# Two token tiles ahead of the first weight half, and the first K products formed half by half

## The chip, the cores and the metric

The kernel runs on one core of one Trainium2 chip. The metric is the device time of one execution in microseconds (us). Each run also has a span (first to last instruction on the core) and a mean granted clock of TensorE, 1.000 being full speed.

## The reference, cut to what matters

```
h  = x  + attention(layernorm(x))        # S = 2048 tokens, D = 1024
h2 = h  + ffn(layernorm(h))              # F = 3584
attention: qkv = layernorm(x) @ wqkv; 32 heads; phi(t) = where(t > 0, t + 1, exp(t)) + 1e-6
           kv = sum over tokens of phi(k)^T v; o = phi(q) kv / (phi(q) z); o @ wo
ffn:       relu(h W_gate) * (h W_up) @ W_down
```

Only the beginning matters here: layernorm of x, K = layernorm(x) @ wk, V = layernorm(x) @ wv.

## The kernel before: the parts that matter

The 16 tiles of 128 tokens are numbered here in the order in which they are processed. Four tiles make a unit. For each tile, `ln_T` computes statistics on VectorE, two tiny functions on ScalarE (Ln, Exp), a "bias" -mean*rstd on VectorE (128x1), the normalised tile `xn` on ScalarE, and its transpose `xT`, by TensorE for the first tiles and by a transposing DMA for the others.

Unit 0 is done with plain matmuls: first K of its four tiles (`k_plain`), then V of its four tiles (`v_plain`). From unit 1 on, a unit is done by Strassen's scheme (`k_unit`, then `v_unit`), which needs sums of its transposed tiles ("left sums", VectorE, of type f16) and sums of the weights ("right sums").

```
        load_x(atiles[0])                # 256 KB, one token tile, rows of 2 KB
        load_w(wk_sb, 0, D)              # 1 MB, left 512 columns of wk, pieces of 1 KB: "K-left"
        load_x(atiles[1])
        load_w(wk_sb, 1, D)              # "K-right"
        load_x(atiles[2])
        load_x(atiles[3])
        for j in range(2):
            load_w(wv_sb, j, 2 * D)
        # ... cut
        def transpose_in(t, xn):
            s, i, r = place(t)
            for k in range(2):
                pt = pspool.tile([P, KH, P], BF16, tag="D", bufs=1, name="tp")   # one PSUM buffer
                for kc in range(KH):
                    nc.tensor.transpose(pt[:, kc, :], xn[:, (k * KH + kc) * P:(k * KH + kc + 1) * P], ident[:])
                (nc.scalar.copy if k else nc.vector.tensor_copy)(
                    out=xT[s][i][:, k * KH:(k + 1) * KH, r:r + P], in_=pt[:])
        # ... cut
        with tc.high_priority():
            # ... SPIN matmuls on zeros, then
            ln_T(atiles[0])
        ln_T(atiles[1])
        todo = atiles[2:8]
        for t in units[0]:
            k_plain(t)                   # both halves of the tile's K
            ln_T(todo.pop(0))
        new_v(0)
        for n, t in enumerate(units[0]):
            v_plain(t)
            if todo:
                ln_T(todo.pop(0))
            if n == 1:
                sums_unit(1)             # left sums of unit 1
                k_sums()                 # right sums of wk
        for u in range(1, NU):
            # ... k_unit(u), with ln_T of the next unit's tiles between its steps;
            # ... u == 1: right sums of wv; kv products of unit u-1; v_unit(u), with the left sums of unit u+1
```

A scheduler decides in which order the instructions of each engine are issued, by times of its own. What is written above only limits it.

Of the kernel before, what the change touches and what calls it, by code (L numbers as in the profile page):

```python
# [7 lines left out]
ACT = mybir.ActivationFunctionType  # L8
ALU = mybir.AluOpType
FP32 = mybir.dt.float32  # L10
BF16 = mybir.dt.bfloat16
# [20 lines left out]
def block_kernel(ctx: ExitStack, tc: tile.TileContext, x, wqkv, wo, wg, wu, wd, out, H: int):  # L32
    nc = tc.nc
    P = 128
    xf = x.flatten_outer_dims()
    of = out.flatten_outer_dims()
    S, D = xf.shape
# [6 lines left out]
    NW = 512  # L44
# [3 lines left out]
    KH = KC // 2  # L48
# [45 lines left out]
    bwork = pqctx.enter_context(tc.tile_pool(name="bwork", bufs=2, side="right"))  # L94
# [32 lines left out]
    def right_ops(w, t):  # L127

        (b11, b12), (b21, b22) = [[w[:, k * KH:(k + 1) * KH, j * NW:(j + 1) * NW] for j in range(2)] for k in range(2)]
        t1, t2, t4, t3 = t[:, 0], t[:, 1], t[:, 2], b12.bitcast(FP16)  # L130

        def sums():
            nc.vector.tensor_tensor(out=t1, in0=b12, in1=b11, op=ALU.subtract)
            nc.vector.tensor_tensor(out=t2, in0=b22, in1=t1, op=ALU.subtract)
            nc.vector.tensor_tensor(out=t3, in0=b22, in1=b12, op=ALU.subtract)
            nc.vector.tensor_tensor(out=t4, in0=b21, in1=t2, op=ALU.subtract)

        return (b11, b21, b22, t4, t1, t2, t3), sums
# [88 lines left out]
    pspool = psctx.enter_context(tc.tile_pool(name="ps", bufs=1, space=PSUM))  # L227
    with ExitStack() as actx:
# [11 lines left out]
        def load_x(t):  # L240
            x_sb = bwork.tile([P, D], BF16, tag=("x_res", "oT")[atiles.index(t) % 2], bufs=XB, name="x_sb")
            nc.sync.dma_start(out=x_sb[:], in_=xf[t * P:(t + 1) * P, :])
            x_tiles[t] = x_sb

        def load_w(dst, j, col):
            nc.sync.dma_start(out=dst[:, :, j * NW:(j + 1) * NW], in_=wqkv_v[:, :, col + j * NW:col + (j + 1) * NW])

        def place(t):
            i, r = divmod(t * P, HS)
            s, r = divmod(r, SW)  # L250
            return s, i, r
# [2 lines left out]
        units = [[2 * u + v + i * ST // 2 for i in range(2) for v in range(2)] for u in range(ST // 4)]  # L254
        atiles = [t for u in units for t in u]
        load_x(atiles[0])
        load_w(wk_sb, 0, D)
        load_x(atiles[1])
        load_w(wk_sb, 1, D)
        load_x(atiles[2])  # L260
        load_x(atiles[3])
        for j in range(2):
            load_w(wv_sb, j, 2 * D)

        def ln_T(t):
            if t not in x_tiles:
                load_x(t)
            x_sb = x_tiles.pop(t)
            s, i, r = place(t)
            stats = asmall.tile([P, 2, nc.vector.BN_STATS_DIM], FP32, tag="stats", name="stats")  # L270
            for k in range(2):
                nc.vector.bn_stats(out=stats[:, k, :], in_=x_sb[:, k * NW:(k + 1) * NW])
            mv = asmall.tile([P, nc.vector.BN_AGGR_DIM], FP32, tag="mv", name="mv")
            nc.vector.bn_aggr(out=mv[:], in_=stats[:])
            sm = asmall.tile([P, 3], FP32, tag="sma", name="sma")
            lnv, rstd, nmr = (sm[:, k:k + 1] for k in range(3))
            nc.scalar.activation(out=lnv, in_=mv[:, 1:2], func=ACT.Ln, bias=LN_EPS, scale=1.0)
            nc.scalar.activation(out=rstd, in_=lnv, func=ACT.Exp, scale=-0.5)
            xn = bwork.tile([P, D], BF16, tag="hn", bufs=HB, name="xn")
            if t == atiles[0]:  # L280
                for k in range(2):
                    ks = slice(k * NW, (k + 1) * NW)
                    nc.vector.tensor_scalar(out=xn[:, ks], in0=x_sb[:, ks], scalar1=mv[:, 0:1], scalar2=rstd,
                                            op0=ALU.subtract, op1=ALU.mult)
                transpose_in(t, xn)
                return
            nc.vector.scalar_tensor_tensor(out=nmr, in0=mv[:, 0:1], scalar=-1.0, in1=rstd, op0=ALU.mult, op1=ALU.mult)
            nc.scalar.activation(out=xn[:], in_=x_sb[:], func=ACT.Identity, bias=nmr, scale=rstd)
            if t not in atiles[:PE_T]:
                nc.sync.dma_start_transpose(out=xT[s][i][:, :, r:r + P], in_=xn[:])  # L290
                return
            transpose_in(t, xn)

        def transpose_in(t, xn):
            s, i, r = place(t)
            for k in range(2):
                pt = pspool.tile([P, KH, P], BF16, tag="D", bufs=1, name="tp")
                for kc in range(KH):
                    nc.tensor.transpose(pt[:, kc, :], xn[:, (k * KH + kc) * P:(k * KH + kc + 1) * P], ident[:])
                (nc.scalar.copy if k else nc.vector.tensor_copy)(  # L300
                    out=xT[s][i][:, k * KH:(k + 1) * KH, r:r + P], in_=pt[:])

        rk, k_sums = right_ops(wk_sb, tk)
# [16 lines left out]
        def new_pk(t):  # L320
            slot = atiles.index(t) % KC
            pk[t] = wo_mem[:, slot * D:(slot + 1) * D]
# [13 lines left out]

            return token_unit(u, rk, fin)

        def k_plain(t):
            s, i, r = place(t)  # L340
            new_pk(t)
            e = bwork.tile([P, D], BF16, tag="o_sb", name="e")
            for j in range(2):
                js = slice(j * NW, (j + 1) * NW)
                ps = pspool.tile([P, NW], FP32, tag="AE"[j], bufs=2, name="kp")
                for kc in range(KC):
                    nc.tensor.matmul(ps[:], lhsT=xT[s][i][:, kc, r:r + P], rhs=wk_sb[:, kc, js],
                                     start=(kc == 0), stop=(kc == KC - 1))
                nc.scalar.activation(out=e[:, js], in_=ps[:], func=ACT.Exp)
                nc.vector.tensor_scalar(out=e[:, js], in0=e[:, js], scalar1=1.0, scalar2=PHI_EPS,  # L350
                                        op0=ALU.min, op1=ALU.add)
                nc.vector.scalar_tensor_tensor(out=pk[t][:, js], in0=ps[:], scalar=0.0, in1=e[:, js],
                                               op0=ALU.max, op1=ALU.add)

        def new_v(u):
            for t in units[u]:
                vs[t] = awork.tile([P, KC, NDW], BF16, tag="v_sb", bufs=5, name="v_sb")
                nc.gpsimd.memset(vs[t][:, :, P:NDW], 1.0)

        def v_plain(t):  # L360
            s, i, r = place(t)
            for j in range(2):
                ps = pspool.tile([P, NW], FP32, tag="AE"[j], bufs=2, name="vp")
                for kc in range(KC):
                    nc.tensor.matmul(ps[:], lhsT=xT[s][i][:, kc, r:r + P], rhs=wv_sb[:, kc, j * NW:(j + 1) * NW],
                                     start=(kc == 0), stop=(kc == KC - 1))
                nc.scalar.copy(out=vs[t][:, j * KH:(j + 1) * KH, 0:P], in_=ps[:].rearrange("p (c e) -> p c e", e=P))
# [21 lines left out]
        def sums_unit(u):  # L389
            s, _, r = place(units[u][0])  # L390
            left_sums(xT[s], xS[s], slice(r, r + 2 * P), nc.vector)
# [3 lines left out]
        with tc.high_priority():  # L395
# [3 lines left out]
            for n in range(SPIN):  # L399
                nc.tensor.matmul(spin[:], lhsT=zero[:, 0:P], rhs=zero[:], start=True, stop=True)  # L400
            ln_T(atiles[0])
        ln_T(atiles[1])
        todo = atiles[2:8]
        for t in units[0]:
            k_plain(t)
            ln_T(todo.pop(0))
        new_v(0)
        for n, t in enumerate(units[0]):
            v_plain(t)
            if todo:  # L410
                ln_T(todo.pop(0))
            if n == 1:
                sums_unit(1)
                k_sums()
        for u in range(1, NU):
            todo = atiles[4 * u + 4:4 * u + 8]
            for _ in k_unit(u):
# [19 lines left out]
        for c in range(KC):  # L437
            bnk, i = divmod(c, GPB)
            nc.vector.tensor_tensor(out=kvz[:, c, :], in0=kv_ps[bnk][:, i * NDW:(i + 1) * NDW],
                                    in1=mask[:], op=ALU.mult)  # L440
# [159 lines left out]
    last = rest[-2:]  # L600
# [314 lines left out]
    prv, k = None, 0  # L915
    for r, (wt, f, fi, toks) in enumerate(runs):
        w = [ops() for _, ops in now]
        later = []
        for n, s in enumerate(toks):
            first = n == 0 and isinstance(wt, int) and fi == 0  # L920
# [50 lines left out]
            if k == nwin - 3:  # L971
                for x in range(2):
                    t = wpools[1].tile([P, KC * 2 * GP * P], BF16, tag=("wg", "wu")[x], name="wd")
# [16 lines left out]
    for n in range(2):  # L990
        t = fpool.tile([P, 4 * D], BF16, tag="wraw", bufs=2, name="xd")
# [346 lines left out]
@with_exitstack  # L1338
def kernel(
    ctx: ExitStack,  # L1340
    tc: tile.TileContext,
    A_x: bass.AP,
    A_wqkv: bass.AP,
    A_wo: bass.AP,
    B_x: bass.AP,
    B_W_gate: bass.AP,
    B_W_up: bass.AP,
    B_W_down: bass.AP,
    out: bass.AP,
):  # L1350
    block_kernel(tc, A_x, A_wqkv, A_wo, B_W_gate, B_W_up, B_W_down, out, H=32)
# [30 lines left out]
```

## Time and profile before

| | |
|---|---|
| time, first three runs | 740.93 us median (740.51 to 741.72) |
| time, six more runs beside the changed kernel | 740.58 us median (739.56 to 741.72) |
| span of the profiled run | 739.5 us |
| first K matmul, first V matmul | 9.96 us, 27.29 us |
| V stage of unit 0 | 27.29 to 41.10 us: 13.81 us |
| K matmuls of unit 1 | 41.10 to 56.59 us: 15.49 us |

Head of the page and busy time of each engine:

```profile
span 739.5 us, 10552 instructions
PE 724.0 (98%) x3967; PEld 382.7 (52%) x4020; DVE 563.7 (76%) x992; ACT 321.5 (43%) x580; POOL 5.6 (1%) x44
```

TensorE (PE) is busy 98% of the span, so a start of some 30 us can give back a few microseconds at most. The timeline of TensorE before; the columns are start, duration, engine, line, operation, output and inputs, count, and in brackets the idle time before it with what ended it:

```profile
7.09 0.39 PE L299 MATMUL tp<-ident,xn 128*128 128x128 bf16 x4
...
9.58 0.58 PE L299 MATMUL tp<-ident,xn 128*128 128x128 bf16 x4 [2.10 <-DVE xT L300]
9.96 3.18 PE L347 MATMUL kp<-pq_mem,xT 128*128 128x512 bf16 x7
...
27.29 0.38 PE L365 MATMUL vp<-wv_sb,xT 128*128 128x512 bf16 x1
```

TensorE waits 2.10 us for VectorE's copy of the first half of tile 0. The seven K matmuls from 9.96 take 3.18 us, about twice what eight of them take elsewhere (1.89 us). The view by stretches of time before says why; its columns are the stretch, its length, busy time and count on PE, weight loads, VectorE (DVE), ScalarE (ACT) and POOL, then the granted clock, the DMA engines' busy share and GB/s:

```profile
2.50:3.50 1.00, 1.00 (x4) 0.39 (x3) 0.00 (x0) 0.00 (x0) 0.07 (x2) 1.00 0.96 352
3.50:4.50 1.00, 1.00 (x3) 0.30 (x2) 0.80 (x2) 0.00 (x0) 0.00 (x0) 1.00 1.08 383
4.50:5.50 1.00, 1.00 (x4) 0.38 (x3) 0.69 (x2) 0.20 (x2) 0.00 (x0) 1.00 1.06 351
...
9.60:13.00 3.40, 3.40 (x12) 1.48 (x12) 1.38 (x2) 1.82 (x3) 0.00 (x0) 0.50 1.07 362
48.00:54.00 6.00, 5.67 (x28) 2.58 (x27) 6.00 (x14) 4.13 (x8) 0.00 (x0) 1.00 0.33 66
54.00:58.00 4.00, 3.95 (x42) 2.80 (x42) 4.00 (x11) 3.94 (x7) 0.50 (x4) 1.00 0.43 97
```

From 9.6 to 13.0 the granted clock was 0.50. The first three rows show the loads running at 351 to 383 GB/s.

The last piece of before that the argument needs is the middle of unit 1, as the timeline shows it on all engines (SPq is the queue that issues the transposing DMAs):

```profile
38.50 0.22 DVE L287 SCALAR_TENSOR_TENSOR sma<-mv,sma 128x1 f32<-128x1 f32 x2
...
41.91 1.32 SPq L290 DMA_TRANSPOSE xT<-xn  x1
...
43.38 0.16 DVE L287 SCALAR_TENSOR_TENSOR sma<-mv,sma 128x1 f32<-128x1 f32 x1
...
44.84 7.22 SPq L290 DMA_TRANSPOSE xT<-xn  x2
...
48.77 0.69 DVE L117 TENSOR_TENSOR xS<-xT 128x1024 f16<-128x1024 bf16 x1
49.37 0.16 DVE L287 SCALAR_TENSOR_TENSOR sma<-mv,sma 128x1 f32<-128x1 f32 x1
...
49.56 1.24 ACT L288 ACTIVATE xn<-x_sb,sma 128x1024 bf16<-128x1024 bf16 x1 [1.38 <-DVE sma L287]
...
51.32 1.89 PE L314 MATMUL Aq<-pq_mem,xT 128*128 128x512 f16 x8 [0.33 <-ACT u L154]
```

Read it as a chain. The biases of tiles 9 and 10 are computed at 38.50, that of tile 11 at 43.38 and that of tile 12 at 49.37. The transpose of tile 10 is issued at 41.91 and that of tile 11 at 44.84; the latter lands at 48.16. The first left sum of unit 2, which needs tiles 8 to 11 transposed, starts at 48.77 without waiting, and TensorE waits only 0.33 us.

### The profile page before, as it was taken

To read this page: it belongs to the slowest core of one execution; us is meant where nothing else is said; L and a number is where in the kernel's file an instruction comes from. 1 tells how busy PE (TensorE), PEld (TensorE's weight loads), DVE (VectorE), ACT (ScalarE), POOL (GpSimd) and SP (SyncE) were. 2 spreads that over 40 slices of the span, in tenths; PEclk is the share of its full clock that TensorE was granted. 3 is DMA by queue.
4 is the path that set the end of the run, shared out by engine and by line. 5 is a ranking of instruction groups with operands and counts; after the bars stand their busy time and mean duration, and the time that the engine had idled before them with its cause. 6 is when DMAs were issued, how large, how long until landed. Compare 5 with 4: busy or idle time off the path is not lost.

```text
span 739.5 us, 10552 instructions
## 1 busy us (share of the span) xinstructions
PE 724.0 (98%) x3967; PEld 382.7 (52%) x4020; DVE 563.7 (76%) x992; ACT 321.5 (43%) x580; POOL 5.6 (1%) x44
## 2 busy tenths in 40 slices
PE   8999999999999999999999999999999999999997
PEld 3444555444444444444444444444444458888566
DVE  5997644676798767778778777877786479996797
ACT  4877554778887644434344444444445120000000
POOL 0000000000000000000000000000000000000000
PEclk9999999999999999999999999999999999999999
DMA  9666002169987426164638359575583399987822
GB/s 315 153 145 170 1 1 67 48 149 218 237 168 181 124 73 206 43 193 134 198 117 242 110 177 283 171 219 194 170 277 121 129 398 339 331 288 299 295 76 82
DMA packets 146594, 132.02 MB, mean 179 GB/s; under 512 B 50928, under 2 KB 128112, under 8 KB 146544
## 3 DMA queue, kind: packets, MB, share of 16 engines
q1 hardware_dynamic: 135536, 123.30, 55.4%
q10 hardware_dynamic: 11008, 8.06, 3.4%
q8 instruction: 31, 0.51, 0.3%
q14 instruction: 19, 0.16, 0.1%
HBM read 79.95 MB, written 39.85 MB: 162 GB/s over the span
## 4 chain that ended last, share of the span: by engine, by line
PE 78%; DVE 8%; ACT 7%; DMA 5%; issue 1%; SPq 0%; DVEq 0%; POOL 0%; ACTq 0%
PE accA L821 22%; PE accY L821 8%; PE accX L821 8%; PE accA L1153 8%; PE Aq L314 3%; PE accA L982 3%; PE attn L557 3%; PE accX L1153 3%; PE Aq L454 3%; PE accY L1153 2%; DMA hn<-hn 2%; ACT hn L570 2%; PE Eq L314 2%; PE accY L982 2%; PE accX L982 2%
## 5 line engine op out<-in xcount | busy, mean ns | idle before, releaser
L831 ACT ACTIVATE gu<-gu 128x512 bf16<-128x512 bf16 x72 | 45.4, 631 | 131.4 <-DVE gu L830 131.4
L826 ACT COPY snap<-accA 128x1024 f32<-128x1024 f32 x72 | 72.5, 1008 | 36.4 <-PE accA L821 36.3
L821 PEld LDWEIGHTS <-tu 128*128 128x128 f16 x384 | 37.6, 98 | 45.3
L821 PEld LDWEIGHTS <-tg 128*128 128x128 f16 x384 | 37.6, 98 | 45.3
L557 PE MATMUL attn<-wo_mem,oT 128*128 128x512 bf16 x247 | 58.1, 379 | 2.3 <-DVE o_sb L534 1.0
L830 DVE TENSOR_TENSOR gu<-accY,snap 128x1024 bf16<-128x1024 f32 x36 | 43.9, 1220 | 10.0 <-ACT snap L826 10.0
L821 PE MATMUL accA<-hn,tu 128*128 128x512 f16 (+1 forms) x192 | 49.3, 379 | 0.0
L821 PE MATMUL accA<-hn,tg 128*128 128x512 f16 (+1 forms) x192 | 49.3, 379 | 0.0
L830 DVE TENSOR_TENSOR gu<-accX,snap 128x1024 bf16<-128x1024 f32 x36 | 43.9, 1219 | 6.3 <-PE accX L821 3.7
L154 ACT COPY u<-Aq 128x512 f32<-128x512 f32 x54 | 31.1, 580 | 36.2 <-PE Aq L314 19.3
L1153 PEld LDWEIGHTS <-x 128*128 128x128 f16 (+1 forms) x448 | 43.8, 98 | 5.5
L821 PEld LDWEIGHTS <-wg 128*128 128x128 bf16 x288 | 28.2, 98 | 34.0
L821 PEld LDWEIGHTS <-wu 128*128 128x128 bf16 x288 | 28.2, 98 | 34.0
L557 PEld LDWEIGHTS <-oT 128*128 128x128 bf16 x256 | 24.6, 97 | 32.2 <-issue 4.1
L834 DVE TENSOR_TENSOR hq<-gu 128x512 bf16<-128x512 bf16 x48 | 20.3, 423 | 14.3 <-ACT gu L831 14.2
L314 PEld LDWEIGHTS <-xT 128*128 128x128 bf16 (+1 forms) x192 | 18.6, 98 | 23.8 <-issue 2.4
L534 DVE TENSOR_TENSOR o_sb<-nd,rd 128x384 bf16<-128x384 f32 (+1 forms) x48 | 23.2, 509 | 8.6 <-ACT rd L533 6.6
L1153 PEld LDWEIGHTS <-xs 128*128 128x128 f16 x280 | 27.4, 98 | 3.2
L982 PEld LDWEIGHTS <-x 128*128 128x128 bf16 (+1 forms) x168 | 16.5, 98 | 19.6
L560 DVE SCALAR_TENSOR_TENSOR x_res<-attn,x_res 128x512 bf16<-128x512 f32 x32 | 22.0, 686 | 6.1 <-PE attn L557 5.9
L1159 DVE TENSOR_TENSOR snap<-accA,u 128x1024 f32<-128x1024 f32 x16 | 19.5, 1220 | 8.0 <-PE accA L1153 7.9
L821 PE MATMUL accA<-hn,wu 128*128 128x512 bf16 x96 | 24.6, 379 | 0.0
(234 smaller groups left out, 1406.1 us busy)
## 6 DMA issues: line engine op xcount, KB each, us to landing
x<-x_dram SPq DMA_DIRECT2D x17, 896.0 KB, 8.1
x_dram<-hq SPq DMA_DIRECT2D x28, 512.0 KB, 3.0
wg<-in_B_W_gate_dram SPq DMA_DIRECT2D x14, 512.0 KB, 5.1
wu<-in_B_W_up_dram SPq DMA_DIRECT2D x14, 512.0 KB, 7.3
wraw<-in_B_W_down_dram SPq DMA_DIRECT2D x14, 512.0 KB, 4.8
x_dram<-hq SPq DMA_DIRECT2D x28, 256.0 KB, 2.5
t_dram<-wt SPq DMA_DIRECT2D x28, 256.0 KB, 2.2
xd<-x_dram SPq DMA_DIRECT2D x6, 896.0 KB, 7.3
```

Source lines behind the costliest of these rows:

```text
L154: nc.scalar.copy(out=snaps[nm, v], in_=bank[v][:])
L314: nc.tensor.matmul(ps[:], lhsT=left[m - 1][:, kc, r + v * P:r + (v + 1) * P], rhs=right[m - 1][:, kc, :], start=(start and kc == 0), stop= ...
L454: nc.tensor.matmul(ps[:], lhsT=rq[m - 1][:, kc, (c + v) * P:(c + v + 1) * P], rhs=left[m - 1][:, kc, :], start=(start and kc == 0), stop=( ...
L534: nc.vector.tensor_tensor(out=ov[:, c0:c0 + n], in0=ndv[:, :, 0:P].rearrange("p k (h e) -> p k h e", h=HPC), in1=rd[:, 0:n, :].unsqueeze(3 ...
L557: nc.tensor.matmul(ps[:], lhsT=st["oT"][:, c, :], rhs=wo_sb[:, c, j * NW:(j + 1) * NW], start=(c == 0), stop=(c == KC - 1))
L560: nc.vector.scalar_tensor_tensor(out=h_sb[:, j * NW:(j + 1) * NW], in0=ps[:], scalar=1.0, in1=h_sb[:, j * NW:(j + 1) * NW], op0=ALU.mult, ...
L821: nc.tensor.matmul(ps[:, v, :], lhsT=w[v][n - 1][:, kc, :], rhs=left[n - 1][:, kc, :], start=(t is not None and kc == 0), stop=(kc == KH - ...
L826: nc.scalar.copy(out=st[nm][:], in_=halves(st["A"]))
L830: add(out=g[:], in0=halves(st[nm]), in1=st[base][:], op=ALU.add)
L831: nc.scalar.activation(out=g[:, 0, :], in_=g[:, 0, :], func=ACT.Relu)
L982: nc.tensor.matmul(ps[:, t * NW:(t + 1) * NW], lhsT=x_tile(n, s, kh)[:, f, (t0 + t) * P:(t0 + t + 1) * P], rhs=w_tile(n, kh)[:, f, :], sta ...
L1153: nc.tensor.matmul(pv[:, tt, :], lhsT=left(m)[:, f, tt * P:(tt + 1) * P], rhs=right(m)[:, f, :], start=(t is not None and f == 0 and tt % ...
```

## The change

The intent was to shorten the start. The load of the second token tile is put ahead of K-left, so that VectorE can do its statistics early. K of the first two tiles is formed left half first, so that TensorE has work while K-right is still on its way. Tile 0's two transposed halves get a PSUM buffer each and are both copied by ScalarE, so that neither waits behind VectorE's statistics. Order-only edges pin a few instructions of VectorE and ScalarE.

```
         load_x(atiles[0])
+        load_x(atiles[1])
         load_w(wk_sb, 0, D)
-        load_x(atiles[1])
+        load_x(atiles[2])
         load_w(wk_sb, 1, D)
-        load_x(atiles[2])
         load_x(atiles[3])
# ... in ln_T: xn of tile 1 in two halves; the instructions' handles are kept in `last` for the edges
+            for ks in [slice(k * NW, (k + 1) * NW) for k in range(2)] if t == atiles[1] else [slice(0, D)]:
+                nc.scalar.activation(out=xn[:, ks], in_=x_sb[:, ks], func=ACT.Identity, bias=nmr, scale=rstd)
# ... in transpose_in
-                pt = pspool.tile([P, KH, P], BF16, tag="D", bufs=1, name="tp")
+                first = t == atiles[0]
+                pt = pspool.tile([P, KH, P], BF16, tag="DE"[k and first], bufs=1 + (k and first), name="tp")
-                (nc.scalar.copy if k else nc.vector.tensor_copy)(
+                last["copy"] = (nc.scalar.copy if k or first else nc.vector.tensor_copy)(
# ... k_plain takes the halves to form; the schedule of unit 0
-        ln_T(atiles[1])
         todo = atiles[2:8]
         for t in units[0]:
-            k_plain(t)
-            ln_T(todo.pop(0))
+            if t == atiles[0]:
+                k_plain(t, [0])
+                with tc.issue_after(last["xn"].ins), tc.issue_after(last["copy"].ins):
+                    ln_T(atiles[1])
+                with tc.issue_after(last["nmr", atiles[1]].ins):
+                    ln_T(todo.pop(0))
+            elif t == atiles[1]:
+                k_plain(t, [0])
+                k_plain(atiles[0], [1])
+                k_plain(t, [1])
+                ln_T(todo.pop(0))
+            else:
+                k_plain(t)
+                ln_T(todo.pop(0))
# ... in the V stage
-                k_sums()
+                with tc.issue_after(last["nmr", atiles[2]].ins):
+                    k_sums()
```

More of the change, by code (lines that the diff above doesn't have):

```diff
@@ L263, in block_kernel @@
             load_w(wv_sb, j, 2 * D)
+        last = {}
         def ln_T(t):
@@ L282, in ln_T @@
                     ks = slice(k * NW, (k + 1) * NW)
-                    nc.vector.tensor_scalar(out=xn[:, ks], in0=x_sb[:, ks], scalar1=mv[:, 0:1], scalar2=rstd,
-                                            op0=ALU.subtract, op1=ALU.mult)
+                    last["xn"] = nc.vector.tensor_scalar(out=xn[:, ks], in0=x_sb[:, ks], scalar1=mv[:, 0:1],
+                                                         scalar2=rstd, op0=ALU.subtract, op1=ALU.mult)
                 transpose_in(t, xn)
                 return
-            nc.vector.scalar_tensor_tensor(out=nmr, in0=mv[:, 0:1], scalar=-1.0, in1=rstd, op0=ALU.mult, op1=ALU.mult)
-            nc.scalar.activation(out=xn[:], in_=x_sb[:], func=ACT.Identity, bias=nmr, scale=rstd)
+            last["nmr", t] = nc.vector.scalar_tensor_tensor(out=nmr, in0=mv[:, 0:1], scalar=-1.0, in1=rstd,
+                                                            op0=ALU.mult, op1=ALU.mult)
+            for ks in [slice(k * NW, (k + 1) * NW) for k in range(2)] if t == atiles[1] else [slice(0, D)]:
+                nc.scalar.activation(out=xn[:, ks], in_=x_sb[:, ks], func=ACT.Identity, bias=nmr, scale=rstd)
             if t not in atiles[:PE_T]:
@@ L337, in k_unit, with k_plain @@
             return token_unit(u, rk, fin)
-        def k_plain(t):
+        ke = {}
+        def k_plain(t, halves=range(2)):
             s, i, r = place(t)
-            new_pk(t)
-            e = bwork.tile([P, D], BF16, tag="o_sb", name="e")
-            for j in range(2):
+            if t not in ke:
+                new_pk(t)
+                ke[t] = bwork.tile([P, D], BF16, tag="o_sb", name="e")
+            e = ke[t]
+            for j in halves:
                 js = slice(j * NW, (j + 1) * NW)
```

## The prediction

> **What bounds the kernel.** By the page TensorE is busy 98% of a 739.5 us span; after about 74 us the chain of waits is nearly all matmuls. The change touches only the first 30 us. In the two builds every engine issues the same sequence after roughly 80 us.
>
> Where TensorE loses time at the start (timeline and windows of before):
> - Spin matmuls run until 7.26. The first half of tile 0 is transposed at 7.09 to 7.48, but VectorE copies it out only at 9.16, behind the statistics of x1 (landed 7.71; 1.29 us) and their aggregate. Both halves share one PSUM buffer, so TensorE waits 2.10 us.
> - From 9.6 to 13.0 the granted clock is 0.50; seven K matmuls start every 0.425 us instead of 0.216: 1.5 us lost. The Trainium skill ("TensorE: Matmul & The Clock Gate", Part 1) says that an idle window of about 3.4 us halves the clock and a busy one restores it. The trace agrees: idle from 7.5 to 9.6, half clock, full again at 13.0.
>
> V starts at 27.3. VectorE is busy without a gap from 13.7 to 38, nearly so to 60, and the chain runs through VectorE, ScalarE's xn and the transposing DMAs until 74. TensorE idles only 1.7 us from 27 to 74. So the gain must exist on VectorE as well as on TensorE.
>
> **What changes.**  xn of tile 1 becomes two halves (about 0.65 us each, from 1.24); tile 0's first copy goes from VectorE (0.37) to ScalarE (0.56).
> - x1 lands near 4.5 instead of 7.7. K-left comes after it, near 7.7 (was about 7.05). x2 lands near 8.4, K-right near 11.5 (was 10.8), at the measured 345 GB/s.
> - Tile 0: both transposes end near 7.9, ScalarE copies near 8.1 and 8.6, eight left matmuls start near 8.2 (was 9.96). The idle falls to about 0.5 us, so the clock should stay full.
> - VectorE: its idle from 6.5 to 13.7 is 3.5 us. In the new order I count 2.3 (1.1 for ScalarE's ln/exp behind the two copies, 1.2 for x3, which lands near 12.3 as before). With the moved copy, a lead of about 1.6 us.
> - New loss: TensorE's order puts three right matmuls of tile 0 ahead of tile 1's left ones, so it waits for K-right from about 10.2 to 11.5.
>
> Scheduling this by hand with measured durations, V starts at 25.5 to 26.3, 1.0 to 1.8 us earlier; about 1.3 us should survive to the end. Most of the 3.6 us of wait and half clock is not gained: the K-right wait and saturated VectorE take it back.
>
> **Predicted: 739.5 us**, 8 in 10 between 738.4 and 740.6. Faster by over 2%: 1%. Within 2%: 98%. Slower by over 2%: 1%.
>
> **What the profile would show.** Granted clock near 1.0 from 9 to 13; tile 0's left matmuls from about 8.2 at 0.216 us spacing; a TensorE wait ended by the K-right DMA near 11.5; VectorE without gaps from about 12.3; first V matmul at 25.5 to 26.3.
>
> **What would make it wrong.** The clock falls to half again because of the K-right wait: V moves by under 0.5 us. K-left lands later than 8.2: a loss one for one. The lead dies in the V stage or unit 1, where the transposing DMAs (about 3.1 us each) or the reordered V sums set the pace: no gain at the end. Or the pinned order saves more VectorE idle than I count: up to 2.5 us gained.

## The result, and the profile after

Ratios in this document are the mean time of one kernel's fast runs over the mean of the other's fast runs of the same rounds, so they are not quite the ratio of the medians quoted beside them. Brackets are 95% intervals. All outputs are right.

| | before | after |
|---|---|---|
| median of 6 runs each | 740.58 us | 745.22 us |
| lowest, highest | 739.56, 741.72 us | 742.93, 746.33 us |
| ratio | | 1.006 [1.0043, 1.0077] |
| first K matmul (profiled run) | 9.96 us | 8.92 us |
| first V matmul | 27.29 us | 26.36 us |
| K matmuls of unit 1 | 15.49 us | 19.50 us |

The change lost 4.6 us by the medians. It is within 2%, but far above the predicted range of 738.4 to 740.6. The changed kernel's six runs roughly follow the clock that was granted: for example 742.93 us at 1.000, 744.80 at 0.998, 745.44 at 0.997, 746.33 at 0.995.

Head of the page of the changed kernel:

```profile
span 743.0 us, 10607 instructions
PE 726.4 (98%) x4020; PEld 382.7 (52%) x4020; DVE 564.0 (76%) x991; ACT 322.9 (43%) x582; POOL 5.8 (1%) x44
```

Work is the same on every engine to within 2.4 us. (The higher count of TensorE instructions is mostly records missing from the trace of before: its 4020 weight loads had 3967 matmul records.) The timeline of TensorE after:

```profile
7.05 0.61 PE L304 MATMUL tp<-ident,xn 128*128 128x128 bf16 x8
8.92 1.89 PE L356 MATMUL kp<-pq_mem,xT 128*128 128x512 bf16 x8 [1.26 <-ACT sma L280]
...
12.61 0.81 PE L356 MATMUL kp<-pq_mem,xT 128*128 128x512 bf16 x3 [1.58 <-DMA pq_mem<-in_A_wqkv_dram]
...
26.36 1.46 PE L374 MATMUL vp<-wv_sb,xT 128*128 128x512 bf16 x6
```

The eight transposes of tile 0 now run in one go. The K matmuls then wait 1.26 us. The profile puts that wait down to ScalarE's Exp, which had long been done; the matmuls start when K-left lands, at 8.9. In a second profile of the same kernel (run e7 below) the same wait is put down to the DMA of K-left. The next wait, 1.58 us, is for K-right, which landed at 12.6.

The stretches of time after:

```profile
2.50:3.50 1.00, 1.00 (x4) 0.39 (x3) 0.15 (x1) 0.00 (x0) 0.07 (x2) 1.00 1.06 395
3.50:4.50 1.00, 1.00 (x3) 0.30 (x2) 1.00 (x2) 0.00 (x0) 0.00 (x0) 1.00 0.35 90
4.50:5.50 1.00, 1.00 (x4) 0.38 (x3) 0.46 (x3) 0.41 (x2) 0.00 (x0) 1.00 0.81 238
...
9.60:13.00 3.40, 1.82 (x12) 0.91 (x11) 1.86 (x4) 1.92 (x5) 0.00 (x0) 1.00 1.08 357
48.00:54.00 6.00, 3.48 (x20) 1.70 (x19) 3.77 (x9) 2.59 (x6) 0.00 (x0) 0.99 0.11 22
54.00:58.00 4.00, 4.00 (x12) 1.51 (x11) 2.69 (x6) 3.89 (x5) 0.00 (x0) 0.59 0.77 160
```

Three things differ. The loads fall to 90 GB/s from 3.5 to 4.5 us, where before they ran at 383. The clock stays at 1.00 from 9.6 to 13.0, as I had predicted. And from 48 to 54 TensorE stands still for 2.5 of 6 us, after which the clock is at half: 0.59 over 54 to 58, in a window that the records place at 53.9 to 57.3.

The middle of unit 1 after:

```profile
42.00 0.22 DVE L289 SCALAR_TENSOR_TENSOR sma<-mv,sma 128x1 f32<-128x1 f32 x2
...
43.45 1.23 SPq L294 DMA_TRANSPOSE xT<-xn  x1
...
45.55 8.15 SPq L294 DMA_TRANSPOSE xT<-xn  x2
...
50.40 0.69 DVE L117 TENSOR_TENSOR xS<-xT 128x1024 f16<-128x1024 bf16 x1 [2.23 <-DMA xT<-xn]
51.01 0.15 DVE L289 SCALAR_TENSOR_TENSOR sma<-mv,sma 128x1 f32<-128x1 f32 x1
...
51.20 1.24 ACT L292 ACTIVATE xn<-x_sb,sma 128x1024 bf16<-128x1024 bf16 x1 [3.12 <-DVE sma L289]
52.34 1.05 ACT L154 COPY u<-Aq 128x512 f32<-128x512 f32 x2
...
52.96 2.71 PE L319 MATMUL Aq<-pq_mem,xT 128*128 128x512 f16 x8 [2.52 <-ACT u L154]
```

The chain of before has become a block. The two biases at 42.00 are those of tiles 10 and 11: tile 10's comes 3.4 us later than before (38.57), tile 11's 1.3 us earlier (43.38). The transpose of tile 10 is issued 1.5 us later (43.45 against 41.91) and that of tile 11 0.7 us later (45.55 against 44.84). Tile 11's also took longer from issue to landing, 4.76 us against 3.33, and lands at 50.31 instead of 48.16. VectorE then reaches the first left sum of unit 2 before its tiles are transposed and waits 2.23 us. Behind it in VectorE's order stands the bias of tile 12, at 51.01. ScalarE's xn of tile 12 waits 3.12 us for that bias. Behind it in ScalarE's order stand the copies that empty TensorE's accumulators. TensorE waits 2.52 us for the copies. The bias stood behind that sum in the kernel before too (sum 48.77, bias 49.37); there the sum did not have to wait.

Where the time went, from these two traces: the first V matmul came 0.93 us earlier, the V stage took 13.81 us in both, and the K matmuls of unit 1 took 4.01 us longer. The sum, +3.1, is what the start of unit 2 shows (72.01 against 68.91), and the spans differ by 3.5. Of the 4.01, 2.2 is the longer wait (2.52 against 0.33) and about 1.7 is half of the 3.4 us window at half clock.

### The profile page after: what moved, and what is told of

The parts are those of the page before. It is cut to its first block, busy times and chain, and to the rows that moved or that the text cites. A ratio compares the mean times of both kernels' runs of the same rounds, so it can differ in the third digit from the quotient of the medians.

```text
span 743.0 us, 10607 instructions
## 1 busy us (share of the span) xinstructions
PE 726.4 (98%) x4020; PEld 382.7 (52%) x4020; DVE 564.0 (76%) x991; ACT 322.9 (43%) x582; POOL 5.8 (1%) x44
## 4 chain that ended last, share of the span: by engine, by line
PE 77%; DVE 9%; ACT 6%; DMA 5%; issue 1%; SPq 0%; DVEq 0%; POOL 0%
PE accA L842 22%; PE accY L842 8%; PE accX L842 8%; PE accA L1174 8%; PE Aq L319 4%; PE accA L1003 3%; PE accX L1174 3%; PE attn L578 3%; PE Aq L475 3%; PE accY L1174 2%; PE Eq L319 2%; ACT hn L591 2%; DMA hn<-hn 2%; PE accY L1003 2%; PE accX L1003 2%
## 5 line engine op out<-in xcount | busy, mean ns | idle before, releaser
L842 PE MATMUL accA<-hs,tg 128*128 128x512 f16 x96 | 24.6, 379 | 0.0
```

What stands on the lines that cost most here:

```text
L842: nc.tensor.matmul(ps[:, v, :], lhsT=w[v][n - 1][:, kc, :], rhs=left[n - 1][:, kc, :], start=(t is not None and kc == 0), stop=(kc == KH - ...
```

## The experiments

**Theories.** T1: the load order made the weights late, and V with them. T2: the scheduler's new order in the V stage and unit 1 made the block. T3, the rival: neither matters, the two profiles differ by the accident of where a half-clock window fell. Each can be true in part.

Several kernels pin instructions with this helper, which lays order-only edges between consecutive instructions of an engine. No wait is taken away by it.

```
+def _order_edges(tc, mark, engine, wanted):
+    traced = [i for i in tc.nc.cur_bb.bb.instructions[mark:] if i.engine == engine]
+    for first, then in wanted:
+        tc.add_manual_dep(traced[then], traced[first].name, <order only>, reason="order")
+        mark = len(tc.nc.cur_bb.bb.instructions)     # ahead of new_v(0), that is ahead of the V stage
+        _order_edges(tc, mark, VectorE, _chain([...]))     # and ScalarE, TensorE
```

Runs e1 to e4 shared one chip and its runs of before (11 runs, median 740.29 us), e5 to e8 the next (739.97), e9 to e12 the last (740.42).

### e1: the changed start with the order of before from the V stage on

```
 # the changed kernel, with
+_order_edges(..., the first 80 VectorE, 60 ScalarE and 200 TensorE instructions from the V stage on, as before had them)
```

> The changed kernel with the issue order of VectorE, ScalarE and TensorE, from the V stage on, put back to that of the kernel before by order edges; the start is the changed one. Theory A (the loss is in the order that the scheduler chose for the stage after the edited one): the first V matmul stays near 26.4, no TensorE wait of 2.5 us near 50, and the time is 739 to 740.2 us, ratio to before 0.998 to 1.000. Rival B (the new start itself costs, through loads or the earlier collisions): 743 to 746, ratio about 1.006.

Measured: 742.11 us, ratio 1.0024 [1.0007, 1.0041]. First V matmul at 27.02. K-left and K-right landed at 9.6 and 13.2, TensorE waiting 2.74 us for the first. K of unit 1 took 15.87 us and no window ran at half clock. So with the old order the block is gone. But the changed start alone does not gain; it loses. The time lies between the ranges of the two theories and meets neither.

### e2: the start of before with the changed kernel's order from the V stage on

```
 # the kernel before, with
+_order_edges(..., the same instructions, in the changed kernel's order)
```

> The kernel before with its own start, and from the V stage on the issue order of the changed kernel forced by the same kind of edges. Theory A: the loss appears without the edited start: 744 to 747 us, ratio 1.004 to 1.008, a TensorE wait of over 2 us near 51 and half clock after it. Rival B: 740 to 741.5, ratio about 1.000.

Measured: 742.56 us, ratio 1.002 [1.0004, 1.0037], again between the two expected ranges. First V matmul at 25.76. Its timeline shows the same block as the changed kernel's:

```profile
49.10 0.69 DVE L130 TENSOR_TENSOR xS<-xT 128x1024 f16<-128x1024 bf16 x1 [2.30 <-DMA xT<-xn]
...
49.90 1.24 ACT L301 ACTIVATE xn<-x_sb,sma 128x1024 bf16<-128x1024 bf16 x1 [3.18 <-DVE sma L300]
...
51.66 3.26 PE L327 MATMUL Aq<-pq_mem,xT 128*128 128x512 f16 x8 [2.59 <-ACT u L167]
```

The late order makes the block by itself, with the old start. Eight matmuls then take 3.26 us, at half clock from 52.0. Its two runs with a clock of 0.999 and more took 740.18 and 740.51 us, no longer than before; the four at 0.997 and 0.998 took 742.41 to 743.39. So the order seems to cost time mostly through the half clock that follows the wait; only one of these six runs was traced.

### e3 and e4: the block's own links

e3 moves the bias of tile 10 ahead of the last three left sums of unit 1. (In the kernel before it also stood ahead of all four right sums of wv; two of these, 46 and 47, still precede it in e3.) e4 puts the bias of tile 12 ahead of the left sum that it stood behind. Both are the changed kernel pinned to its own order but for this.

```
 # e3: VectorE's chain of the changed kernel
-[... 8, 34, 47, 9, 10, 11, 29, ...]        # 8 to 11: left sums of unit 1; 29: the bias of tile 10
+[... 8, 34, 47, 29, 9, 10, 11, ...]
 # e4
-[... 52, 63, 68, 53, 54, 55, ...]     # 52 to 55: left sums of unit 2; 63: the bias of tile 12
+[... 63, 52, 68, 53, 54, 55, ...]
```

> The changed kernel in exactly its order, but VectorE's bias of token tile 10 moved from behind the left sums of unit 1 to ahead of their second. If the late transpose of tile 10 starts the loss: its transpose issues at 42.0 to 42.6 instead of 43.45, tile 11's lands near 49 instead of 50.3, the TensorE wait near 50 falls from 2.5 to about 1.3 us, time 742 to 744. If the position of this one instruction does not matter: 744.5 to 746.

> The changed kernel in exactly its order, but VectorE's bias of token tile 12 moved one place, ahead of the first left sum of unit 2, which waits for the transposing DMA. The transposes stay as late as in the changed kernel. If the cost comes through the in-order queues (VectorE held by that sum, so ScalarE held at xn of tile 12, so its copies of the accumulators and TensorE): the 2.5 us TensorE wait falls below 0.8, the half clock near 55 is gone, time 740 to 742. If the late data itself holds TensorE: no change, 744.5 to 746.

Measured: e3 743.76 us, 1.0045 [1.0024, 1.0066]; e4 743.4 us, 1.0041 [1.0022, 1.0059]. e3 is inconclusive: its first V matmul came at 27.76 because K-left landed late (10.3), the transpose of tile 10 was issued no earlier (43.92; counted from the first V matmul, 0.9 us earlier), and TensorE still waited 2.16 us. In e4 the wait of 2.5 us is gone, so the bias of tile 12 behind the left sum did carry it. No window ran at half clock in this trace, as expected. But a wait of 1.57 us for VectorE came a few matmuls later, and the time did not fall to the expected 740 to 742. Breaking one link moves part of the wait to the next.

### e5: the load order alone

```
 # the kernel before, pinned from the start to its own order on VectorE, ScalarE and TensorE, and
         load_x(atiles[0])
+        load_x(atiles[1])
         load_w(wk_sb, 0, D)
-        load_x(atiles[1])
+        load_x(atiles[2])
         load_w(wk_sb, 1, D)
-        load_x(atiles[2])
         load_x(atiles[3])
```

> The kernel before with only its first loads reordered as in the change (x0, x1, K-left, x2, K-right, x3); the order on VectorE, ScalarE and TensorE is pinned to that of the kernel before. Theory C (the load order itself loses DMA time): between 3.5 and 6 us the traffic dips under 300 GB/s, where the two traces with the old order keep 305 to 389; K-left lands at 8.6 to 10.3 instead of 7.0, K-right at 12.3 to 14 instead of 10.5 to 10.8, the first V matmul moves to 27 to 28.5 and the time is 741.3 to 743.5. Rival (my prediction's arithmetic, K-left at 7.7 and K-right at 11.5 with steady traffic): no dip, first V matmul near 26.3, 740 to 741.

Measured: 745.39 us, ratio 1.0068 [1.0054, 1.0081]. The load order alone, in the old start, costs as much as the whole change, and more than theory C had expected (741.3 to 743.5); the traffic fell under 300 GB/s as it had expected (249 to 272 from 3.5 to 5.5 us). Its timeline of TensorE:

```profile
9.68 1.02 PE L360 MATMUL kp<-pq_mem,xT 128*128 128x512 bf16 x4 [1.18 <-DMA pq_mem<-in_A_wqkv_dram]
...
13.38 1.44 PE L360 MATMUL kp<-pq_mem,xT 128*128 128x512 bf16 x3 [2.67 <-DMA pq_mem<-in_A_wqkv_dram]
...
30.74 13.98 PE L378 MATMUL vp<-wv_sb,xT 128*128 128x512 bf16 x63
```

K-left lands at 9.6 and K-right at 13.3, and a half-clock stretch lies over 11.8 to 18.6 (by estimate, half of these 6.8 us are lost). So part of this price is the waits and part the clock; all six runs had a clock of 0.994 to 0.998. The rest of the change (K left half first, two PSUM buffers) takes back part of what its load order costs: the changed kernel's V came at 26.4, this one's at 30.7.

### e6: the left sums of unit 2 behind everything that others wait for

```
 # the changed kernel pinned to its own order, but for VectorE
-[..., 52, 63, 68, 53, 54, 55, 30, 31, ...]     # 30, 31: the adds of two accumulators
+[..., 63, 68, 30, 31, 52, 53, 54, 55, ...]
```

> The changed kernel in exactly its order, but VectorE's four left sums of unit 2, the first of which waits for the last transposing DMA, moved behind the bias of tile 12 and the two adds of the accumulators that they held up. The transposes stay as late. Theory A' (the loss in unit 1 is head-of-line blocking in the in-order queues): no TensorE wait over 0.6 us between 48 and 56, no half clock there, unit 1 takes 15.7 to 16.4 us instead of 19.5, time about 741 to 742 (what is left is the later start). If late transposes hold the data that TensorE needs: unit 1 stays above 18 us, time 744 to 746.

Measured: 744.03 us, ratio 1.0046 [1.003, 1.0062]. The median missed the expected 741 to 742. Its timeline shows the block gone, and where part of the time was given back:

```profile
49.75 1.89 PE L332 MATMUL Aq<-pq_mem,xT 128*128 128x512 f16 x8
...
59.85 1.89 PE L332 MATMUL Aq<-tv,xS 128*128 128x512 f16 x8 [1.46 <-ACT m L167]
```

K of unit 1 took 14.97 us, the shortest of all runs. Its V part took 14.79 instead of 12.3, with waits of 0.70 and 1.46 us. One of its six runs had a clock of 1.000 and took 742.0 us; the others, at 0.997 and 0.998, took up to 745.27. The profiled run shows no half clock in this stretch, so I have no trace of what lowers it in those runs.

### e7: the changed kernel again

> The changed kernel unaltered, as the reference of this chip: 744 to 746 us, a DMA dip between 3.5 and 6 us, unit 1 about 18 us long, or 19.5 where the clock halves in it; its fastest run, at clock 1.000, near 742.9.

Measured: 743.59 us (741.25 to 744.76), ratio 1.0039 [1.0022, 1.0056]. The fastest run had a clock of 1.000, the slowest 0.997. This is faster than the first set, and than the expected 744 to 746. In this trace K-left landed at 9.5 and K-right at 13.2, V started at 27.00, TensorE's wait in unit 1 was only 1.21 us and there was no half clock. The order is the same; the transpose of tile 11 took 3.45 us to land here, and 4.76 to 4.83 in the other six traces with the changed order (the changed kernel, e2, e3, e4, e6, e10). Why it takes longer in those is not shown. So V in the profiled runs of the changed start (the changed kernel, e1, e3, e4, e6, e7) spreads from 26.0 to 27.8, and the block varies from run to run.

### e8 and e10: K-left second, everything else as changed

```
 # e10: the changed kernel, and
         load_x(atiles[0])
-        load_x(atiles[1])
         load_w(wk_sb, 0, D)
+        load_x(atiles[1])
         load_x(atiles[2])
 # e8: the same, and the order of before from the V stage on, as in e1
```

> The changed kernel with the loads in the order x0, K-left, x1, x2, K-right, x3, its start otherwise in the changed order, and the later order of the kernel before (as in the run of the changed start with the old order, 742.1). Theory C: no dip, K-left lands near 7.0, the left matmuls of tile 0 start near 8.2, first V matmul at 25.2 to 25.9, time 739.3 to 740.3, so about the kernel before or 0.5 us under it. If the load order is not the cause: first V matmul near 26.5 to 27, time 741.5 to 742.5.

> The changed kernel with only the first loads in the order x0, K-left, x1, x2, K-right, x3; by the build, its instruction order on every other engine is that of the changed kernel, the late order too, and nothing is pinned. Theory C with A: no dip, first V matmul at 24.6 to 25.2 (26.1 to 27.8 in the changed kernel), 1.5 to 2.5 us gained on the changed kernel, but the late order still holds TensorE near 50: time 741 to 742.8. If the late order costs nothing once the start is early: 739.5 to 740.5. If the load order is not the cause: 743.5 to 745.

Measured: e8 740.34 us, ratio 1.0002 [0.9987, 1.0017]; e10 741.2 us, ratio 1.0005 [0.999, 1.002]; e10 is in the range of theory C with A, e8 just at the upper end of its own. In e10 the build has exactly the changed kernel's instruction order on all engines but the one that issues the loads; only this order differs. Its timeline of TensorE:

```profile
7.30 1.90 PE L356 MATMUL kp<-pq_mem,xT 128*128 128x512 bf16 x8 [0.36 <-ACT xT L305]
...
11.03 0.81 PE L356 MATMUL kp<-pq_mem,xT 128*128 128x512 bf16 x3 [0.20 <-DMA pq_mem<-in_A_wqkv_dram]
...
24.79 2.97 PE L374 MATMUL vp<-wv_sb,xT 128*128 128x512 bf16 x13
...
50.94 2.68 PE L319 MATMUL Aq<-pq_mem,xT 128*128 128x512 f16 x8 [2.58 <-ACT u L154]
```

and its loads in the second that collapsed in the changed kernel:

```profile
3.50:4.50 1.00, 1.00 (x5) 0.35 (x3) 0.78 (x2) 0.00 (x0) 0.00 (x0) 1.00 1.05 368
```

With K-left second, K-left landed at 6.6 and K-right at 11.0, the two waits shrink to 0.36 and 0.20 us, and V starts at 24.79, 1.6 to 2.2 us earlier than in the two traces of the changed kernel. The interval of e10 just misses e7's, and lies clear of that of the first set (1.0043 to 1.0077), so the loads' order costs the changed kernel about 0.3%, 2 to 3 us. But e10's block is still there, and the half clock after it (51.9 to 55.3). Here too the time followed the clock: the three runs with 0.999 and more took 740.05 to 740.44 us, the three with 0.998, the traced one among them, 741.96 to 742.99. With the old late order, e8 starts V at 24.68 and loses 1.39 us at the start of unit 1, waiting for a transposing DMA. Neither is faster than before beyond its interval: the lead at V, about 0.7 to 1.1 us against the old start without half clock (25.51 in e9, 25.76 in e2), is all or mostly spent in unit 1.

### e9: the kernel before again

> The kernel before unaltered, for a second trace of it. Theory D (the half clock at 9.6 to 13.0 in the trace that I predicted from was an accident of that execution): most runs have a granted clock of 0.999 or 1.000, the profiled one with 7 chances in 10, and then no half clock before 700 us, first V matmul near 25.8 and a span near 738.0. If the half clock belongs to the kernel: clock 0.998, first V matmul near 27.3, span 739.5 again.

Measured: 740.55 us, ratio 1.0002 [0.9989, 1.0015]. The timeline of TensorE in this second trace of the kernel before:

```profile
9.07 0.38 PE L299 MATMUL tp<-ident,xn 128*128 128x128 bf16 x4 [1.29 <-DVE xT L300]
9.29 1.73 PE L347 MATMUL kp<-pq_mem,xT 128*128 128x512 bf16 x7
...
25.51 2.32 PE L365 MATMUL vp<-wv_sb,xT 128*128 128x512 bf16 x10
```

Same program, another execution: seven matmuls in 1.73 us instead of 3.18, no half clock before the kernel's end (737.2), and V at 25.51 instead of 27.29. TensorE's wait for tile 0 was 1.29 us here and 2.10 there: x1, whose statistics VectorE does first, landed at 7.2 instead of 7.7. In each of the three sets of 11 runs of before, 9 or 10 runs had a clock of 0.999 or 1.000. The half-clock window on which I had built the prediction was an accident of the one execution that was profiled.

So the fair pair of traces is e9 and e7, the two kernels without half clock. There the changed kernel's V comes 1.49 us later (27.00 against 25.51), not earlier; unit 1's K takes 0.94 us longer (16.38 against 15.44), and the spans differ by 2.8 us (741.5 against 738.7).

### e11 and e12: why the weights are late

```
 # e11: the kernel before, pinned to its order: x0, x2, K-left, x1, K-right, x3
 # e12: the kernel before, pinned: x0, x1, K-left as two transfers (rows 0-511, 512-1023), x2, K-right, x3
```

> The kernel before, pinned, with loads x0, x2, K-left, x1, K-right, x3, a look at the DMA traffic alone. If two token tiles ahead of K-left make the dip, whichever they are: under 300 GB/s at some time between 3.5 and 6 us and K-left at 8.6 or later. If it is the neighbouring rows of x0 and x1: no dip (x2 lies 1024 rows away), K-left at 7.6 to 7.9.

> The kernel before, pinned, with loads x0, x1, K-left in two transfers of 512 KB, x2, K-right, x3. If the size of the transfer that follows the two tiles makes the dip: steady traffic over 300 GB/s from 3.5 to 6 us and K-left at 7.6 to 8.0. If not: the dip stays, K-left at 8.6 to 10.3.

Measured, one run each, state unknown, both at a clock of 0.995: 744.23 and 745.53 us. In e11, with a token tile that is no neighbour of the first one in memory, the loads never fell under 300 GB/s in half-microsecond slices once they ran (2.5 to 6.0 us), yet K-left landed at 8.9 and TensorE waited 4.12 us for the copy of tile 0. In e12 the dip only moved later (176 GB/s from 5.0 to 5.5 us), and TensorE waited 3.37 us for K-right. Neither run mends the order, e11 fits neither of its two expectations, and together they do not name the cause.

What the traces do show is in the packets. In the records of single 1 KB weight packets of the first 14 us, the median takes 46 to 47 ns. Packets over 100 ns number 1 to 6 in the five traces with K-left directly behind x0 (before, e2, e8, e9, e10), and 18 to 38 in the eight with x0 and x1 ahead of it (the changed kernel, e1, e3 to e7, e12). In e11 they number 12. Single packets take up to 1.1 us (e3). And the loads do not finish in turn. K-left consists of 1024 such packets, yet when it landed 1131 to 1694 of the weights' packets had ended in the nine traces with two token tiles ahead of it (1493 in e11, whose rate never fell), against 1024 to 1141 in the other five: packets of later loads were done while a part of K-left was still missing. Why, stays open.

### Side finding from the builds

Moving the three load lines alone in the kernel before also changes the scheduler's order of VectorE in the V stage and unit 1, so e5 had to be pinned to isolate the loads. Taking away one edge of the change had the same effect. Only the move of e10 left the order alone.

## Why the prediction was wrong, point by point

I predicted 739.5 us; it is 745.2, and 743.6 when measured again.

1. **"K-left comes after it, near 7.7 ... K-right near 11.5 ... at the measured 345 GB/s": the term that was mis-sized.** I added one tile's bytes to the old landing and divided by the old rate. The landings were 8.9 and 12.6 in the profiled run, 8.5 to 10.3 and 12.2 to 14.0 over the traces of the changed start. The rate did not stay (90 GB/s from 3.5 to 4.5 us), and later loads' packets ended ahead of K-left's last ones; in e11 K-left was late, at 8.9, without any fall of the rate. The Trainium skill gives 341 GB/s for a transfer of 1 MB, measured on loads issued from GpSimd ("DMA: Bandwidth & Descriptors", Bandwidth, Measured). The old order of this kernel, issued from SyncE, comes near it (351 to 383 GB/s from 2.5 to 5.5 us); the new one does not. I had named the danger ("K-left lands later than 8.2: a loss one for one") but put it outside the range. e5 shows the load order's cost by itself in the old start (+0.68%), e10 shows it taken away with all else equal (1.0005 against 1.0039).

2. **"From 9.6 to 13.0 the granted clock is 0.50 ... 1.5 us lost": a premise that was an accident.** I counted these 1.5 us as a loss of the kernel, to be won back. e9 has no such window, and V starts at 25.51. My prediction for the changed kernel's V, 25.5 to 26.3, was no gain against that at all. (And the trace that I said agreed with the page had a wait of 2.10 us, not an idle window of 3.4.) The page that I cited says that the window is free-running and that the count of slow matmuls varies from run to run; it advises not to fit to a specific one ("TensorE: Matmul & The Clock Gate", Part 1). I took the first half of that section and not the second. The traces agree with it: the same kernel with and without the window (seven matmuls in 3.18 and in 1.73 us).

3. **"In the two builds every engine issues the same sequence after roughly 80 us" and "about 1.3 us should survive to the end": the step that failed in the middle.** The sentence is true and not enough. Between 27 and 80 us the builds do differ, and I carried a lead through this stretch as if they did not. The changed order computes the bias of tile 10 3.4 us later (42.00 against 38.57); the transposes of tiles 10 and 11 are issued 1.5 and 0.7 us later, the last one also takes 1.4 us longer and lands at 50.31 instead of 48.16, and one VectorE instruction that waits for it holds up ScalarE and TensorE. e2 shows that this order makes the block without the changed start, and costs 0.2% [0.04%, 0.37%]. The Trainium skill says that VectorE and ScalarE take their instructions strictly in order ("Perfetto Trace Analysis", Tensor Engine Instruction); the traces agree: the bias at 51.01, a 128x1 operation of 0.15 us whose input had long been ready, starts right behind the sum that waited 2.23 us. I had named this danger too ("the lead dies in the V stage or unit 1").

4. **Right: tile 0 and the clock at the start.** The transposes of tile 0 run in one go (7.05 to 7.66), the clock is 1.00 from 9.6 to 13.0, TensorE waits for K-right. The mechanism of the start works; e10's V at 24.79 is the gain that it could have had.

How the parts add, from the four combinations (median us and ratio to before):

| loads | order of before in V and unit 1 | changed order |
|---|---|---|
| x0, K-left, x1, x2, K-right | e8: 740.34, 1.0002 | e10: 741.2, 1.0005 |
| x0, x1, K-left, x2, K-right | e1: 742.11, 1.0024 | changed kernel (e7): 743.59, 1.0039 |

The four did not all share a chip, so take the ratios, not the medians. Down a column is the loads' price, 0.22% and 0.34%, or 1.6 and 2.5 us. Along a row is the order's, 0.15% and 0.03%, or 1.1 and 0.2 us. The intervals of e1 and e8, e1 and e7, and e8 and e10 overlap, so these steps are not resolved one by one; that of e10 to e7 is, barely, and e2's interval by itself excludes no effect of the order. T1 is shown, T2 is shown for the block and weakly for the time, and T3 is right for the profile of before and for the run-to-run spread. As the whole explanation T3 is refuted by the runs that had no half clock to speak of: on e7's chip, the nine runs of before with a clock of 0.999 and more took 739.34 to 741.03 us, and the three of the changed kernel 741.25 to 743.33.

Left open: why 1 KB packets slow down behind two token tiles; why e6 has no block in its trace and yet no better median; and the spread of the long part. From the second batch of kv products (about 82 us) to the end the 14 traces take 657.6 to 659.3 us, though the kernels before and after issue the same order there; that spread is as much as several of the effects above.

No version beat the kernel before.

## What to carry to other kernels

Before a half-clock window is booked as a loss, look at the clock of several executions: if most run at 0.999 or more, the window belongs to the execution and not to the kernel. A new load order has a landing time that must be measured, for instance by swapping only the loads; the old rate does not carry over. When an edit moves the order of instructions elsewhere, compare the builds to the last difference, and look on an in-order engine for an instruction that waits for a DMA ahead of a small one that another engine needs. Moving it takes that wait away, as e4 and e6 show; here it did not shorten the kernel, because other waits took its place.

## What the Trainium skill lacked or had wrong

- "DMA: Bandwidth & Descriptors": nothing on how the order of loads changes their rate. With two 256 KB token tiles ahead of a 1 MB weight half in 1 KB pieces, the rate fell to 90 GB/s over 3.5 to 4.5 us (383 with one tile ahead), K-left landed at 8.5 to 10.3 us instead of 6.5 to 7.0, and 18 to 38 packets took over 100 ns (median 46) instead of 1 to 6. In one run, e11, it landed at 8.9 us though the rate stayed over 300 GB/s.
- "DMA: Bandwidth & Descriptors", Latency and other measured facts: it gives an effective rate of 261 GB/s for transposing DMAs with a non-contiguous middle dimension; an estimate from that is 1.0 us for a tile of 128x1024 bf16 (262,144 bytes). From issue to landing such a transpose took 3.1 to 4.8 us in the changed kernel from 30 to 52 us (median 3.6), and 3.0 to 4.1 before (median 3.4). No page has the time of one transpose to landing.
- "TensorE: Matmul & The Clock Gate", Part 1: its table gives half clock after at least one idle window of about 3.4 us. In the 14 traces, from 5 to 62 us, eleven single waits of TensorE were 2.10 us or longer. Eight of them led to half clock, the shortest being 2.10 us (before), and three did not (2.66 in e3, 2.74 in e1, 2.81 in e2). No shorter wait did. So much less than a whole window of idle time was enough. What sorts them in these traces is where the wait fell. In each trace the changes of clock lie whole multiples of 3.413 us apart. On a grid of that step laid through them, the window just ahead of each of the eight half-clock stretches held 2.00 to 2.59 us of TensorE idle time (2.10 in before, 2.49 in the changed kernel), and no other window at full clock before 730 us held more than 1.90 (e1). The three waits without effect were cut by a boundary of the grid, into 1.84 and 0.82 us, 0.84 and 1.90, and 1.13 and 1.68.
- The same page says that the ramp costs under 1% of a typical span. That agrees: one 3.4 us window at half clock loses some 1.7 us of 740, 0.2%. But it has no figure for how far a kernel's whole time spreads between runs: the changed kernel took 742.93 us at a clock of 1.000 and 746.33 at 0.995, 0.5%, more than the gain that was predicted (1.1 us).
